# Who issues one block's decay spread, and in which order one DMA queue loads weights and inputs, in a fused Mamba-2 and ELU kernel

## The chip, the cores and the metric

The kernel runs on one core of a Trainium2 chip. The metric is the device time of one execution in microseconds (us), taken over several executions; the median counts. Lower is better.

## The reference, cut to what matters

```python
# attention part: batch 4, 8 heads, 768 tokens, head_dim 32, d_state 16
log_a = np.log(np.clip(a, 1e-06, 1.0))
...
cum = np.cumsum(la, axis=-1)                         # within a chunk
L = np.exp(cum[:, :, :, None] - cum[:, :, None, :]) * causal
CB = np.einsum('bhin,bhjn->bhij', Cc, Bc)
y_intra = np.einsum('bhij,bhjd->bhid', CB * L, xc)
y_inter = np.einsum('bhin,bhnd->bhid', Cc, state) * np.exp(cum)[:, :, :, None]
y[:, :, sl] = y_intra + y_inter
state = decay_full * state + sum over the chunk of B x decay_from_j
...
# feed-forward part: x is y as (3072 tokens, 256), w_in (256, 2048), w_out (2048, 256)
h = x @ w_in
g = np.where(h > 0.0, h, np.exp(np.minimum(h, 0.0)) - 1.0)
return g @ w_out
```

The two weight matrices come in as 64-bit floats and are turned into 32-bit ones on the chip.

## The kernel before, in words

**Tiling.** The 3072 tokens are cut into twelve blocks of 256, counted from 0 in the code (so the code's block 2 is the third). Each block goes through the attention part (decays, scores, states, output `yT`), then through the first product `l1(n, i)` with eight pieces of `w_in`, the ELU, and the second product `l2(n, i)` with eight pieces of `w_out`. From block 4 on, pairs of blocks go through a scheme with fewer products. PSUM has seven rotating buffers (`p_a`, line 76) for scores, transposes and first products, and one more (`p_o`).

**Order.** The schedule is written out by hand (`manual_schedule`, line 82): each engine, and each DMA queue, runs its instructions in the order of the program text. Lines 867 to 1004 are the start of the kernel, where the first three blocks, the conversion of the weight pieces and the loads are interleaved. Nearly all DMAs are issued by SyncE's queue (SP in the profile), so a DMA that waits, or is slow to issue, holds up those after it in the text.

**Weights.** `w_load(i)` (lines 157 to 160) loads piece i, 512 KB, on SP; pieces 0 to 7 are `w_in`, 8 to 15 `w_out`, in eight rotating buffers. `w_take(i, low)` (line 855) reads the raw piece: an Abs on ScalarE (line 175), a scaling (line 182 on ScalarE or 184 on VectorE), a sign mask on VectorE (line 193). `w_give(i)` finishes it with two VectorE steps (lines 201 and 208) and a sum on GpSimd (line 218), after which `l1` or `l2` can use the piece.

**Decays.** Blocks 0 and 1 get their decays from products on TensorE. For the other blocks the running sums of log a, the tile `F`, are stored to DRAM by `write_flat` (lines 325 to 328: two DMAs to `flat`, one to `flat_exp`) and read back. `spread_cum(n)` (lines 348 to 355) broadcasts block n's running sums over the partitions with two DMAs of 256 KB into the tile `L`; it must wait for `flat`. `spread_exp(n)` (lines 357 to 362) does the same with `flat_exp`, one DMA of 128 KB into `ec`. `decay_of(n, h)` (lines 476 to 486) then turns `L` into decays with two exponentials on ScalarE (line 479), and masks them on GpSimd every fourth head (line 484). `load_bc(n)` loads B and C of a block in four DMAs of 64 KB (line 129) and `load_x(n)` its x in two of 128 KB (line 137).

**Around the change.** In the text, piece 4 is loaded at line 872; then lines 921 to 931 issue, on SP: piece 5, the stores of `write_flat`, piece 6, `spread_cum(2)`, piece 7, B and C of block 2, x of block 2, `spread_exp(2)`, pieces 8 and 9. On ScalarE the ELU of line 951 is followed by `w_take(4, nc.scalar)` (line 956), the `yT` copies of block 1 in `inside(across(1), 1)` (line 958; the copies are line 610 on ScalarE and 608 on VectorE), the ELU of line 963 and then the loop of lines 968 to 1004. That loop interleaves, per step s, one first product, `decay_of(2, s)` for s up to 7, the next weight piece (every second step) and one ELU. After step 5 it turns B and C of block 2 (`turn(2)`, `turn_exp(2)`: copies and masks of lines 391, 394 and 402), and at step 7 it computes the scores of block 2 (line 499), whose four PSUM buffers come free when those copies and the ELUs before them are done.

Of the kernel before, what the change touches and what calls it, by code (L numbers as in the profile page):

```python
# [28 lines left out]
def kernel(  # L29
# [27 lines left out]
    nc = tc.nc  # L57
# [21 lines left out]
    def psum(shape, name):  # L79
        return p_a.tile(shape, F32, tag="a", name=name)  # L80
# [21 lines left out]
    def rows_of(n):  # L102
        b, g = place(n)
        return slice(NG * NH * b + g, NG * NH * (b + 1), NG)

    def load_bc(n, c_queue=nc.sync):
        b, g = place(n)
        st.setdefault(n, {})["bc"] = raw.tile([P, 2, 2, NH, N], F32, tag="bc", name="bc", bufs=2)
        if n > 3:
            st[n]["b"] = raw.tile([P, 2, NH, N], F32, tag="b", name="b_tok", bufs=2)  # L110
            for u in range(2):
                sl = slice((2 * g + u) * P, (2 * g + u + 1) * P)
                nc.sync.dma_start(
                    out=st[n]["b"][:, u], in_=B[b, :, sl, :].rearrange("h s n -> s h n"))


            squares = st[n]["bc"].rearrange("p k u h n -> p k (u h n)").rearrange(
                "p k (m r) -> p k m r", m=2)
            for k, src in enumerate((B, C)):
                for m in range(2):  # L120
                    nc.sync.dma_start(
                        out=squares[:, k, m],
                        in_=src[b, m:NH:2, g * BLK:(g + 1) * BLK, :].rearrange(
                            "q (c t) n -> q c (t n)", t=8))
            return
        for u in range(2):
            sl = slice((2 * g + u) * P, (2 * g + u + 1) * P)
            for k, src in enumerate((B, C)):
                (nc.sync, c_queue)[k].dma_start(  # L129
                    out=st[n]["bc"][:, k, u], in_=src[b, :, sl, :].rearrange("h s n -> s h n"))  # L130

    def load_x(n):
        b, g = place(n)
        st[n]["x"] = raw.tile([P, 2, NH * D], F32, tag="xr", name="xr", bufs=4)
        for u in range(2):
            sl = slice((2 * g + u) * P, (2 * g + u + 1) * P)
            nc.sync.dma_start(  # L137
                out=st[n]["x"][:, u].rearrange("p (h d) -> p h d", d=D),
                in_=x[b, :, sl, :].rearrange("h s d -> s h d"))
# [17 lines left out]
    def w_load(i):  # L157
        if i < len(pieces):
            w_raw[i] = conv.tile([P, 2, 2 * CW], U32, tag="w64", name="w64", bufs=W_AHEAD)
            nc.sync.dma_start(out=w_raw[i], in_=pieces[i][1])  # L160
# [11 lines left out]
    def w_abs(i):  # L172
        w_mag[i] = (ffn.tile([P, 2, CW], U32, tag="tmp", name="mag", bufs=1) if i == 2 else
                    conv.tile([P, 2, CW], U32, tag="mag", name="mag"))
        nc.scalar.activation(w_mag[i].bitcast(F32), w_words(i)[1].bitcast(F32), ACT.Abs)
# [4 lines left out]
    def w_low(i, eng):  # L180
        if eng is nc.scalar:
            eng.activation(pieces[i][0], w_words(i)[0], ACT.Identity, scale=2.0 ** -51, bias=two)
        else:
            eng.tensor_scalar(
                out=pieces[i][0], in0=w_words(i)[0], scalar1=2.0 ** -51, scalar2=2.0,
                op0=ALU.mult, op1=ALU.add)
# [3 lines left out]
    def w_sign(i, cols=slice(None)):  # L190
        if i not in w_sgn:
            w_sgn[i] = conv.tile([P, 2, CW], U32, tag="sgn", name="sgn")
        nc.vector.tensor_scalar(  # L193
            out=w_sgn[i][:, :, cols], in0=w_words(i)[1][:, :, cols], scalar1=0x80000000,
            scalar2=None, op0=ALU.bitwise_and)

    def w_high_a(i, cols=slice(None)):
        mag = w_mag[i][:, :, cols]


        nc.vector.tensor_scalar(
            out=mag.bitcast(F32), in0=mag.bitcast(F32),
            scalar1=high_word_as_f32(0x38000000), scalar2=high_word_as_f32(0x47EFFFFF),
            op0=ALU.max, op1=ALU.min)
# [120 lines left out]
    def write_flat():  # L325
        for v in range(2):
            nc.sync.dma_start(out=flat[v], in_=F[:, 0, :, Q * v:Q * v + Q])
        nc.sync.dma_start(out=flat_exp, in_=F[:, 1].rearrange("r u i -> r (u i)"))
# [16 lines left out]
    state = {}  # L345
    starts = {}

    def spread_cum(n):

        st.setdefault(n, {})["L"] = L = att.tile([P, NH, 2, Q], F32, tag="L", name="L", bufs=2)  # L350
        for v in range(2):
            nc.sync.dma_start(
                out=L[Q * v:Q * v + Q].rearrange("p h u i -> p h (u i)"),
                in_=flat[v, rows_of(n)].rearrange("h u i -> h (u i)").unsqueeze(
                    0).to_broadcast([Q, NH, P]))

    def spread_exp(n):

        st.setdefault(n, {})["ec"] = ec = att.tile([P, 2, P], F32, tag="ec", name="ec", bufs=4)
        nc.sync.dma_start(  # L360
            out=ec.rearrange("p u i -> p (u i)"),
            in_=flat_exp[rows_of(n)].unsqueeze(1).to_broadcast([NH, N, BLK]))
# [142 lines left out]
    def weigh(n, q):  # L505
        s = st[n]
        M = att.tile([P, 2, 2, Q], F32, tag="M", name="M", bufs=8)
        nc.vector.tensor_tensor(
            out=M, in0=s["g"][q],
            in1=s["L"][:, 2 * q:2 * q + 2].rearrange("p k u i -> p u k i"), op=ALU.mult)  # L510
        s["M"].append(M)
# [105 lines left out]
    def l1(n, i, parts=1):  # L617

        ps = psum([P, 2, BLK], "ps_h")
        for j in range(2):  # L620
            m = 2 * i + j
            for part in range(parts):
                toks = slice(part * BLK // parts, (part + 1) * BLK // parts)
                for k in range(KC):
                    nc.tensor.matmul(  # L625
                        out=ps[:, j, toks], lhsT=w_in[:, k, m * P:(m + 1) * P],
                        rhs=yT[n // 2][:, k, n % 2].rearrange("p u i -> p (u i)")[:, toks],
                        start=(k == 0), stop=(k == KC - 1))
        lag.append((n, i, ps))
# [10 lines left out]
    def elu():  # L640
        if not begun:
            begin_elu()
        n, i, ps = lag.pop(0)
        e = begun.pop()
        nc.scalar.activation(e, e, ACT.Exp, scale=-1.0)  # L645
        g_of[n, i] = ffn.tile([P, 2, BLK], F32, tag=f"g{n % 2}", name="g", bufs=12)
        nc.vector.scalar_tensor_tensor(  # L647
            out=g_of[n, i], in0=e, scalar=1.0, in1=ps,
            op0=ALU.subtract, op1=ALU.max)
# [205 lines left out]
    def w_take(i, low):  # L855

        w_abs(i)
        w_low(i, low)
        w_sign(i)
# [58 lines left out]
    w_sign(2)  # L918
    w_give(2)
    elu()  # L920
    w_load(5)
    nc.scalar.activation(F[:, 1], F[:, 0], ACT.Exp)
    write_flat()
    w_load(6)
    spread_cum(2)
    w_load(7)
    load_bc(2)
    load_x(2)
    spread_exp(2)
    w_load(8)  # L930
    w_load(9)
    first_low(1, p_o)
# [20 lines left out]
    weigh(1, 2)  # L953
    weigh(1, 3)
    l1(0, 3)
    w_take(4, nc.scalar)
    w_high_a(4)
    inside(across(1), 1)
# [9 lines left out]
    for s, (n, i) in enumerate((  # L968
# [19 lines left out]
        if s == 8:  # L988
            spread_cum(3)
            load_x(3)  # L990
            spread_exp(3)
            weigh(2, 2)
            weigh(2, 3)

            st[0] = kept
            sums(2, 0, pool=p_o, tag="o", parts=(None, last))
            states(0, last)
            st.pop(0)
            states(2)
        if s == 10:  # L1000
            spread_cum(4)
            inside(across(2), 2)
# [197 lines left out]
    n = NP - 2  # L1200
# [41 lines left out]
```

## Time and profile before

| | us |
|---|---|
| median of 3 runs | 357.2 |
| lowest and highest of them | 357.05 and 357.94 |
| the profiled execution, its own time | 359.15 |
| its span on the core | 357.4 |
| PE (TensorE products) busy | 349.0 (98%) |
| DVE (VectorE) busy | 241.3 (67%) |
| POOL (GpSimd) busy | 231.1 (65%) |
| ACT (ScalarE) busy | 200.9 (56%) |

All times in the profile are microseconds from the start of the span. The granted TensorE clock is full throughout. A row of the timeline view has the start, the duration, the engine, the line of the kernel, the operation, the tile written and those read, and how many instructions were merged into the row; brackets give how long the engine sat idle before it, and what ended that. `SPq` and `ACTq` are the two queues that issue DMAs; their rows show the issuing of a DMA, not the flow of its data. A row of the waits view has who waited for whom, the sum, the number of waits and the longest.

### The profile page before, as it was taken

How to read it: one execution, taken by the hardware profiler on the slowest of the kernel's cores; microseconds unless marked ns; L12 is line 12 of the kernel's file. 1: busy time of each engine (PE TensorE's matmuls, PEld its weight loads, DVE VectorE, ACT ScalarE, POOL GpSimd, SP SyncE). 2: the span in 40 equal slices, each digit the busy share in tenths (PEclk: the TensorE clock that was granted, in tenths of full speed). 3: DMA queues.
4: the chain of work that ended last, by engine and by line, in shares of the span. 5: the costliest groups of instructions: out<-in, count | busy, mean ns of one | idle time of the engine just before them, and what ended most of it. 6: DMA issues, size and time to landing. Idle time of an engine off the chain costs nothing.

```text
span 357.4 us, 9940 instructions
## 1 busy us (share of the span) xinstructions
PE 349.0 (98%) x3960; PEld 313.3 (88%) x3960; DVE 241.3 (67%) x500; ACT 200.9 (56%) x491; POOL 231.1 (65%) x365
## 2 busy tenths in 40 slices
PE   8799899999999999999999999999999999999995
PEld 5578688888888999899999999999899999999995
DVE  4996996994799768784577685586685465656212
ACT  4776969867625476635586635486635444434000
POOL 5552553564766998769568769568669545465983
PEclk9999999999999999999999999999999999999999
DMA  8887998380450500046600047500000100000001
GB/s 139 214 249 148 205 327 177 79 141 31 61 147 3 119 0 3 8 89 130 134 0 2 8 72 148 132 5 0 2 2 4 59 3 0 2 0 31 30 2 60
DMA packets 82878, 26.49 MB, mean 74 GB/s; under 512 B 59728, under 2 KB 78736, under 8 KB 82832
## 3 DMA queue, kind: packets, MB, share of 16 engines
q1 hardware_dynamic: 80656, 25.67, 32.0%
q8 instruction: 31, 0.51, 0.6%
q10 hardware_dynamic: 2176, 0.20, 0.5%
q14 instruction: 15, 0.12, 0.1%
HBM read 22.51 MB, written 3.34 MB: 72 GB/s over the span
## 4 chain that ended last, share of the span: by engine, by line
PE 90%; SPq 4%; DVE 2%; DMA 1%; ACT 1%; issue 0%; POOL 0%; DVEq 0%; ACTq 0%
PE ps_o L807 35%; PE ps_h L697 27%; PE ps_h L625 13%; PE ps_o L746 8%; PE ps_y L593 2%; SPq L129 2%; PE ps_g L499 2%; PE ps_y L574 1%; DMA w<-in_moe_w_in_dram 1%; PE ps_st L529 1%; DVE g L647 1%; SPq L160 1%; SPq L137 0%; SPq L88 0%; DVE sgn L193 0%
## 5 line engine op out<-in xcount | busy, mean ns | idle before, releaser
L638 ACT ACTIVATE e<-ps_h 128x512 f32<-128x512 f32 x96 | 57.0, 593 | 91.1 <-DVE ps_h L722 44.1
L807 PEld LDWEIGHTS ps_o<-w_out,g 128*128 128x128 f32 x640 | 79.9, 192 | 3.1 <-issue 0.5
L807 PE MATMUL ps_o<-w_out,g 128*128 128x128 f32 x640 | 80.9, 275 | 0.0
L647 DVE SCALAR_TENSOR_TENSOR g<-e,ps_h 128x512 f32<-128x512 f32 x96 | 65.1, 679 | 11.5 <-ACT e L645 11.5
L625 PE MATMUL ps_h<-yT,w_in 128*128 128x256 f32 (+1 forms) x272 | 60.9, 371 | 2.6 <-POOL w_in L218 2.6
L645 ACT ACTIVATE e<-e 128x512 f32<-128x512 f32 x96 | 61.0, 635 | 2.0
L774 POOL TENSOR_TENSOR g<-g 128x256 f32<-128x256 f32 x33 | 23.9, 726 | 54.5 <-DVE g L647 54.4
L625 PEld LDWEIGHTS ps_h<-yT,w_in 128*128 128x128 f32 x272 | 48.3, 190 | 10.3 <-POOL w_in L218 3.9
L807 PE MATMUL ps_o<-w_sum,g 128*128 128x128 f32 x320 | 42.9, 275 | 0.0
L479 ACT ACTIVATE L<-L,ncum 128x64 f32<-128x64 f32 x160 | 41.0, 337 | 3.0 <-DMA L<-flat 3.0
L807 PEld LDWEIGHTS ps_o<-w_sum,g 128*128 128x128 f32 x320 | 41.1, 192 | 1.2
L697 PE MATMUL ps_h<-yT,w_in 128*128 128x256 f32 x128 | 38.8, 385 | 0.0
L730 DVE TENSOR_TENSOR ps_h<-ps_h,u_sum 128x512 f32<-128x512 f32 x32 | 22.3, 698 | 23.5 <-PE ps_h L697 23.4
L697 PE MATMUL ps_h<-y_sum,w_in 128*128 128x256 f32 x128 | 38.1, 380 | 0.0
L697 PE MATMUL ps_h<-y_sum,w_sum 128*128 128x256 f32 x128 | 38.1, 380 | 0.0
L484 POOL TENSOR_SCALAR_AFFINE_SELECT L<-L 64x512 f32<-64x512 f32 x40 | 28.6, 714 | 10.9 <-ACT L L479 9.6
L714 DVE TENSOR_TENSOR u_sum<-ps_h,u_sum 128x512 f32<-128x512 f32 x32 | 22.1, 690 | 14.5 <-ACT u_sum L707 8.1
L722 DVE TENSOR_TENSOR ps_h<-ps_h,u_sum 128x256 f32<-128x256 f32 x32 | 13.8, 432 | 26.3 <-PE ps_h L697 26.3
L746 PE MATMUL ps_o<-w_out,g 128*128 128x256 f32 x128 | 30.8, 384 | 0.0
L762 POOL TENSOR_TENSOR t<-g 128x256 f32<-128x256 f32 x40 | 28.9, 752 | 0.3
L762 POOL TENSOR_TENSOR g<-g,t 128x256 f32<-128x256 f32 x40 | 28.8, 752 | 0.2
L762 POOL TENSOR_TENSOR g<-t,g 128x256 f32<-128x256 f32 x40 | 27.9, 731 | 1.1 <-PE ps_o L807 1.1
(109 smaller groups left out, 531.9 us busy)
## 6 DMA issues: line engine op xcount, KB each, us to landing
L<-flat SPq DMA_DIRECT2D x20, 256.0 KB
w<-in_moe_w_in_dram SPq DMA_DIRECT2D x8, 512.0 KB
w<-in_moe_w_out_dram SPq DMA_DIRECT2D x8, 512.0 KB
xr<-in_x_dram SPq DMA_DIRECT2D x24, 128.0 KB
out_dram<-c_sum SPq DMA_DIRECT2D x10, 256.0 KB
bc<-in_B_dram SPq DMA_DIRECT2D x24, 64.0 KB
bc<-in_C_dram SPq DMA_DIRECT2D x22, 64.0 KB
ec<-flat_exp SPq DMA_DIRECT2D x10, 128.0 KB
```

Of the source, the lines that this page charges most:

```text
L479: nc.scalar.activation(L[:, h, u], L[:, h, u], ACT.Exp, bias=ncum[:, u, row:row + 1])
L484: nc.gpsimd.affine_select(out=part, in_=part, pattern=[[0, 4], [0, 2], [1, Q]], compare_op=ALU.is_ge, fill=0.0, base=0, channel_multiplier=-1)
L625: nc.tensor.matmul(out=ps[:, j, toks], lhsT=w_in[:, k, m * P:(m + 1) * P], rhs=yT[n // 2][:, k, n % 2].rearrange("p u i -> p (u i)")[:, toks],
L638: nc.scalar.activation(begun[0], lag[0][2], ACT.Relu, scale=-1.0)
L645: nc.scalar.activation(e, e, ACT.Exp, scale=-1.0)
L647: nc.vector.scalar_tensor_tensor(out=g_of[n, i], in0=e, scalar=1.0, in1=ps, op0=ALU.subtract, op1=ALU.max)
L697: nc.tensor.matmul(out=out, lhsT=lhsT, rhs=rhs, start=first, stop=True, skip_group_check=True)
L730: nc.vector.tensor_tensor(out=c2, in0=c2, in1=u[:, 0:2], op=ALU.add)
L746: nc.tensor.matmul(out=o_of[n][:, ts], lhsT=g_of[n, j][:, m % 2, ts * P:(ts + 1) * P], rhs=w_out[:, m], start=(m == 0 and ts == 0), stop=( ...
L762: nc.gpsimd.tensor_tensor(out=out, in0=in0, in1=in1, op=ALU.subtract)
L774: eng.tensor_tensor(out=b12, in0=b12, in1=b11, op=ALU.subtract)
L807: nc.tensor.matmul(out=ps[:, ts], lhsT=b[:, ts * P:(ts + 1) * P], rhs=a[:, i], start=(i == chunk[0] and ts == 0), stop=(i == chunk[-1]), s ...
```

## The change

The spread of block 2's running sums is issued from ScalarE's queue, and stands in the text after `l1(0, 3)` instead of between pieces 6 and 7. `spread_exp(2)` moves to the same place but stays on SP, so that there it comes after piece 9. The stores of `write_flat` come ahead of piece 5; piece 6 still comes ahead of B and C of block 2, and piece 7 now after that block's x. The SP order thus becomes: piece 4, stores, piece 5, piece 6, B and C of block 2, x of block 2, pieces 7, 8 and 9, `spread_exp(2)`, B and C of block 3.

```diff
-    def spread_cum(n):
+    def spread_cum(n, queue=nc.sync):
...
         for v in range(2):
-            nc.sync.dma_start(
+            queue.dma_start(
...
     elu()
-    w_load(5)
     nc.scalar.activation(F[:, 1], F[:, 0], ACT.Exp)
     write_flat()
+    w_load(5)
     w_load(6)
-    spread_cum(2)
-    w_load(7)
     load_bc(2)
     load_x(2)
-    spread_exp(2)
+    w_load(7)
     w_load(8)
     w_load(9)
     first_low(1, p_o)
...
     l1(0, 3)
+    spread_cum(2, nc.scalar)
+    spread_exp(2)
     w_take(4, nc.scalar)
     w_high_a(4)
     inside(across(1), 1)
```

## The prediction

> **What bounds the kernel now.** I read the page first: PE is busy for 98% of the span, so only the few places where TensorE waits can give anything. The waits view of PE over the whole run ends with three rows, and from 55 us on it has none: what TensorE gains or loses before 55 us reaches the end one for one. So I read the waits between 18 and 56 us:
>
> ```profile
> ACT L L479 <- DMA L<-flat: 3.0, 1, 3.0
> ...
> PEld ps_g L499 <- ACT e L638: 1.5, 2, 1.2
> ...
> PE ps_g L499 <- DVE ctm L394: 0.8, 1, 0.8
> ...
> PE ps_h L625 <- POOL w_in L218: 0.6, 2, 0.4
> ```
>
> ScalarE waits 3.0 us for block 2's running sums to land. TensorE waits at that block's scores (line 499), and a little for a weight piece. The timeline of PE shows where and how long:
>
> ```profile
> 38.69 1.89 PE L625 MATMUL ps_h<-yT,w_in 128*128 128x256 f32 x8
> 40.97 1.99 PE L625 MATMUL ps_h<-yT,w_in 128*128 128x256 f32 x8 [0.39 <-POOL w_in L218]
> 43.79 1.51 PE L499 MATMUL ps_g<-ctm,bct 32*64 32x128 f32 x32 [0.82 <-DVE ctm L394]
> 45.23 1.99 PE L625 MATMUL ps_h<-yT,w_in 128*128 128x256 f32 x8
> ```
>
> Undisturbed, a first product takes 1.73 us from start to start (56.28 to 58.01) and 32 score products 0.62 (block 3's: 65.45 to 66.07). So the last row could start at 38.69 + 2 x 1.73 + 0.62 = 42.77. It starts at 45.23: **2.46 us** can be won, no more. Why are the scores late? The timeline of ACT:
>
> ```profile
> 22.88 0.63 ACT L645 ACTIVATE e<-e 128x512 f32<-128x512 f32 x1
> 23.41 0.66 ACT L175 ACTIVATE mag<-w 128x512 f32<-128x512 f32 x1
> 23.97 0.75 ACT L182 ACTIVATE w_in<-w,two 128x512 f32<-128x512 uint32 x1
> 26.62 0.81 ACT L610 COPY yT<-ps_y 128x128 f32<-128x128 f32 x3 [1.90 <-PE ps_y L593]
> 27.45 0.60 ACT L638 ACTIVATE e<-ps_h 128x512 f32<-128x512 f32 x1
> 28.08 0.63 ACT L645 ACTIVATE e<-e 128x512 f32<-128x512 f32 x1
> 31.72 1.06 ACT L479 ACTIVATE L<-L,ncum 128x64 f32<-128x64 f32 x4 [3.01 <-DMA L<-flat]
> ```
>
> From 31.72 to 47.9 ScalarE has no gap in its timeline: it carries the 3 us as a backlog. VectorE takes its work from it (g and the weight masks), and the scores' four PSUM buffers and `ctm` come from VectorE, g of (1, 3) last, at 44.58. Why does the spread land at 31.72? The issues on SP:
>
> ```profile
> 16.31 3.79 SPq L160 DMA_DIRECT2D w<-in_moe_w_in_dram  x2
> 20.21 1.33 SPq L327 DMA_DIRECT2D flat<-F  x2
> 21.64 0.54 SPq L328 DMA_DIRECT2D flat_exp<-F  x1
> 22.24 0.46 SPq L160 DMA_DIRECT2D w<-in_moe_w_in_dram  x1
> 24.32 2.41 SPq L352 DMA_DIRECT2D L<-flat  x2
> 26.78 0.97 SPq L160 DMA_DIRECT2D w<-in_moe_w_in_dram  x1
> ```
>
> The stores are queued behind pieces 4 and 5 (the first issue is held until 19.59), SP then waits until 24.32 for them to land, and issues the two spreads in 2.41. From the last issue's end (26.73) to ScalarE's start is 5.0 us.
>
> **What the Trainium skill says.** "Perfetto Trace Analysis", section on the HWDGE DMA instruction: its semaphore wait is on the sequencer, and the descriptor generator is then locked while it is used. So ScalarE's stream stops at the spread until `flat` has landed and both are issued. The same page, section on DVE and Act instructions: the sequencer pushes an ACTIVATE into a wait queue and goes on. The trace agrees: a DMA was issued on ACT's queue at 1.74 while its table load ran from 1.71 to 2.99. "DMA: Bandwidth & Descriptors", section "Issuing engines are not separate DMA queues": another issuer saves only its sequencer's issue time, the data share the same 16 engines. No row of before tests this beyond the start. The same page, "Queues, rings and completion order": an engine takes turns between the queues that have work. So the spread would no longer stand behind piece 6 but share with pieces 5 and 6.
>
> **The change part by part.**
>
> *Stores ahead of piece 5.* Their source is ready (the sums precede the exponential, which ends at 17.3), so SP issues them at 19.7 to 21.0, then `flat_exp` to 21.6. Before, the landing came 2.8 us after their issue ended (21.54 to 24.32), with 512 KB of piece 5 ahead; at the 315 to 389 KB per us that the DMA engines moved from 21 to 24 us this is some 1.5 us, if all of it was still to flow. So `flat` is there between 21.0 + 1.3 = 22.3 and 21.0 + 2.8 = 23.8; I take 23.2.
>
> *Spread on ScalarE's queue.* Two issues of the spread row's median 0.63 us each: 23.2 to 24.5. Line 175 starts at 24.5 instead of 23.41, 1.1 us later, and ends at 25.2, line 182 at 25.8. Behind them stand the `yT` copies at 26.62, ahead of which ScalarE sat idle for 1.90: the 1.1 is hidden. VectorE's step on piece 4 starts at 26.42 and needs line 175 at 25.2: hidden too. **Cost 0**, as long as the issues end by about 25.3. If they take as long as the slow spread before (0.73 and 1.68), they end at 25.6, and cost 0.3. If SP's stall on the third B/C DMA of block 2 (3.05 us in before) holds the generator for both queues, ACT comes free near 27.5 and the cost is 27.5 - 25.3 = 2.2. Below nothing it can't be: nothing in this stretch of TensorE waits on the queue. I take 0 and keep 2.2.
>
> *When L lands.* 24.5 + 5.0 (before's delay) = 29.5. The bounds: 2.8 (the stores' delay) gives 27.3; if pieces 5 and 6, 1 MB, all flow ahead of it, 1.5 us more gives 31.0. I take 29.5: ScalarE's wait shrinks from 3.0 to 0.8, so its work starts 2.2 us earlier.
>
> *What is late next.* ScalarE copies the transposed B of block 2 at 40.87; TensorE writes it from 38.25 for 0.38, ending at 38.63. So ScalarE can be early by no more than 40.87 - 38.63 = 2.2 there, even if L came sooner. Shifting g of (1, 3) from 44.58 by 2.2 gives 42.4 (TensorE gets there at 42.15), and g of (0, 5), which frees the buffer for the next first product, from 45.16 to 43.0. The product at 45.23 thus starts at 43.0: **gain 2.2 us**. The wait for a weight sum (0.39) goes with it.
>
> *Piece 5 later.* Issued at 21.7 to 22.2 instead of 19.6 to 20.1, landing near 25 to 26; VectorE reads it at 29.60. 0. If it were 4 us later than that, VectorE would start on it late, but its next step waits for ScalarE at 30.4 anyway.
>
> *B, C and x of block 2 earlier, piece 7 later.* SP no longer spends 1.6 us waiting and 2.41 issuing. B, C and x took 6.8 us of issue before (27.85 to 34.65), so now some 22.7 to 29.7. Piece 7 is issued near 30 instead of 26.8 and lands by 35; its first reader on VectorE moves from 40.59 to about 38.4. 0, with 3 us to spare. Uncovered, each us beyond would delay the `w_in` sum of piece 7, used at TensorE's 45.5.
>
> *`spread_exp(2)` behind pieces 7, 8 and 9.* Issued at some 31 to 36 (34.70 before); with 1.5 MB ahead, at most 4.5 us to flow, it lands by 36 to 41. Its reader, VectorE's line 402, moves from 43.56 to 41.4. 0. At the late end this takes up all the slack.
>
> The sum is 0 - 2.2 = **-2.2 us**. The profiled execution took 359.15 (span 357.4 and 1.75 around it), so it would be 356.95; it stands 1.95 above the median 357.2. The same 2.2 off the median gives **355.0**.
>
> **The rivals.**
>
> *A, as worked out, 0.60.* 355.0, from 354.7 (all 2.46) to 355.6 (0.3 of cost and L 0.3 late).
>
> *B, the wait only shrinks, 0.14.* L shares the DMA engines with pieces 5 and 6 and lands at 30.7: ScalarE gains 1.0, the scores come 1.0 earlier, 356.2. For it: the data rate is 348 to 377 KB per us at 23 to 25 us, so the engines are nearly full then. Against it: at 25 to 26 it falls to 160.
>
> *C, slower, 0.15.* ScalarE's queue is held by SP's: the lock stays with SP through B and C of block 2, which need about 5 us from 22.7, until 27.9. The spreads are then issued until 29.2, so line 175 starts at 29.2 instead of 25.3 at the latest, and TensorE's first product of block 1 (27.48) slips by 3.9. Of that, 2.46 is absorbed by the waits that go: +1.4, 358.6. It decides for slower once the issues end later than 25.3 + 2.46 = 27.8, and then L, at 29.2 + 5.0 = 34.2, is later than before as well. For it: SP's issues stall in just this stretch. Against it: at the start, between 1.70 and 3.0 us, SP and ACT issued two DMAs each at 0.39 to 0.58, with no stall.
>
> *D, no difference, 0.11.* The same hold, but for SP's one stall (27.5): 2.2 lost ahead of block 1, 2.2 won at the scores, 357.2.
>
> **How the numbers follow.** A measurement tells 0.3% (1.07 us) from no change, so faster means below 356.13. A gives 0.60; half of B, which lies on the border, 0.07: 0.67. Slower (above 358.27) is C: 0.15. The rest, D and half of B and what lies between, 0.18. Range: A's low end less 0.4 for the spread between runs, 354.3, to 357.5, which takes in B and D and leaves out C and a few more.
>
> **What would show it.** A issue row of L352 on ACTq near 23 to 24.5; ScalarE's wait before line 479 below 1 us; the score products in about 0.7 us from start to start, starting near 42.2; and the product after them near 43.0. TensorE's first product of block 1 should still start at 27.5. If that slips, C or D is at work; if it holds and ScalarE still waits over 1.5 us for L, it is B. The prediction would also be wrong if TensorE waited anew for a piece or for `ec` between 40 and 55 us.

## The result, and the profile after

The changed kernel takes **362.88 us** (median of 6 runs, 360.82 to 364.18) against 357.45 for the kernel before in the same comparison: a ratio of **1.0139**, 95% interval 1.0105 to 1.0173. It is slower by some 5 us, where a gain of 2.2 was forecast. A later comparison on another chip gave 361.91 and 1.0121 (1.0098 to 1.0145). The profiled execution took 362.95 (span 361.2).

The waits of the changed kernel between 10 and 60 us, longest of those that matter:

```profile
ACT mag L175 <- DMA bc<-in_B_dram: 5.2, 1, 5.2
...
PE ps_h L625 <- ACT yT L610: 4.3, 2, 3.3
...
ACT L L479 <- DMA L<-flat: 1.4, 1, 1.4
```

The wait for L did shrink. In its place ScalarE stands still for 5.2 us ahead of line 175, and TensorE then waits 3.3 us for `yT`. The view names a B DMA as what ended ScalarE's wait, although line 175 reads weight piece 4: what stands ahead of line 175 in ScalarE's stream is the spread. Its timeline:

```profile
22.97 0.63 ACT L645 ACTIVATE e<-e 128x512 f32<-128x512 f32 x1
26.65 2.11 ACTq L352 DMA_DIRECT2D L<-flat  x2
28.81 0.66 ACT L175 ACTIVATE mag<-w 128x512 f32<-128x512 f32 x1 [5.21 <-DMA bc<-in_B_dram]
29.37 0.75 ACT L182 ACTIVATE w_in<-w,two 128x512 f32<-128x512 uint32 x1
30.02 0.79 ACT L610 COPY yT<-ps_y 128x128 f32<-128x128 f32 x3
30.83 0.60 ACT L638 ACTIVATE e<-ps_h 128x512 f32<-128x512 f32 x1
```

The spread was to be issued from 23.2 to 24.5; it is issued from 26.65 to 28.76. Line 175 starts at 28.81 and the `yT` copies at 30.02, with no gap between them: they come late because of the queue alone. SyncE's issues in the same stretch:

```profile
18.83 1.33 SPq L327 DMA_DIRECT2D flat<-F  x2
...
20.85 0.93 SPq L160 DMA_DIRECT2D w<-in_moe_w_in_dram  x2
21.89 0.40 SPq L129 DMA_DIRECT2D bc<-in_B_dram  x1
22.34 0.58 SPq L129 DMA_DIRECT2D bc<-in_C_dram  x1
22.97 3.39 SPq L129 DMA_DIRECT2D bc<-in_B_dram  x1
```

The stores go out at 18.83 to 20.16, as early as forecast. The third B/C DMA is held for 3.39 us until 26.36, which is suspiciously near 26.65. TensorE:

```profile
30.86 13.22 PE L625 MATMUL ps_h<-yT,w_in 128*128 128x128 f32 x64 [3.30 <-ACT yT L610]
43.92 0.38 PE L387 MATMUL ps_tb<-ident,bc 128*128 128x128 f32 x2
...
47.91 0.69 PE L499 MATMUL ps_g<-ctm,bct 32*64 32x128 f32 x32
48.53 1.99 PE L625 MATMUL ps_h<-yT,w_in 128*128 128x256 f32 x8
```

The 64 products, 10.93 us before, take 13.22. Two rows of the view by stretches, whose columns after the busy times end in the granted clock, the DMA share and GB/s, say why:

```profile
29.00:30.00 1.00, 0.00 (x0) 0.00 (x0) 0.43 (x2) 1.00 (x2) 0.00 (x0) 0.63 1.25 201
31.00:32.00 1.00, 1.00 (x5) 1.00 (x6) 1.00 (x3) 0.97 (x2) 0.33 (x1) 0.50 1.13 193
```

While TensorE stands idle its granted clock falls to one half. It is back at full only after 36 us (0.96 from 36 to 37, 1.00 from 37).

**What the spread waited for.** The trace also records every increment of the DMA completion semaphores, and the program as built says which one each DMA uses. There are eight of them, given to the DMAs of both queues in turn, and each DMA waits until the DMA eight before it in that round has landed:

```
the spread's   round in the    DMA eight before            its last    spread's
DMA            changed kernel  in the round                increment   issue
first          34              26, weight piece 6          26.63       26.65
second         36              28, first C of block 2      28.16       28.18
                               (the two stores of flat:    22.28 and 22.46)
```

The stores had landed when ScalarE got there, at 22.98. Nothing else was missing but the landing of piece 6, and then of a C, neither of which the spread reads.

### The profile page after: what moved, and what is told of

The parts are those of the page before. It is cut to its first block, busy times and chain, and to the rows that moved or that the text cites. A ratio compares the mean times of both kernels' runs of the same rounds, so it can differ in the third digit from the quotient of the medians.

```text
span 361.2 us, 9938 instructions
## 1 busy us (share of the span) xinstructions
PE 350.3 (97%) x3960; PEld 315.4 (87%) x3960; DVE 241.8 (67%) x500; ACT 201.2 (56%) x491; POOL 231.6 (64%) x365
## 4 chain that ended last, share of the span: by engine, by line
PE 92%; DMA 3%; SPq 1%; ACT 1%; DVE 1%; POOL 0%; issue 0%; ACTq 0%
PE ps_o L807 35%; PE ps_h L697 27%; PE ps_h L625 15%; PE ps_o L746 8%; PE ps_y L593 2%; DMA bc<-in_C_dram 2%; PE ps_g L499 2%; DMA w<-in_moe_w_in_dram 2%; PE ps_y L574 1%; PE ps_st L529 1%; SPq L129 0%; POOL w_in L218 0%; ACT mag L175 0%; SPq L137 0%; DVE mag L208 0%
## 5 line engine op out<-in xcount | busy, mean ns | idle before, releaser
L625 PE MATMUL ps_h<-yT,w_in 128*128 128x256 f32 (+1 forms) x272 | 63.0, 383 | 5.7 <-ACT yT L610 4.3
L625 PEld LDWEIGHTS ps_h<-yT,w_in 128*128 128x128 f32 x272 | 50.8, 203 | 12.9 <-ACT yT L610 3.5
```

Source lines behind the costliest of these rows:

```text
L625: nc.tensor.matmul(out=ps[:, j, toks], lhsT=w_in[:, k, m * P:(m + 1) * P], rhs=yT[n // 2][:, k, n % 2].rearrange("p u i -> p (u i)")[:, toks],
```

## The experiments

Theory 1: ScalarE's stream stands still until the previous user of the spread's completion semaphore has landed. Theory 2, rival C of the prediction: SyncE's held B/C DMA keeps the descriptor generator from ScalarE. Both fit the first issue in this one trace, since 26.36 and 26.63 are so near.

**Other turns in the round.** The order on both queues stays that of the change; only the turns move:

```diff
     states(1)
+    st[2]["x"] = raw.tile([P, 2, NH * D], F32, tag="xr", name="xr", bufs=4)
+    for u in range(2):
+        nc.gpsimd.memset(st[2]["x"][0:32, u, 0:8], 0.0)
...
     spread_cum(2, nc.scalar)
+    load_x(2)
+    w_load(7)
+    w_load(8)
+    w_load(9)
     spread_exp(2)
```

(the four loads are taken out of their place ahead of `first_low(1, p_o)`; `load_x` uses the tile made here)

> The changed kernel, with both queues in the same order, but x of block 2 and what follows it held back by two tiny GpSimd writes, so that in the round of the eight DMA completion semaphores the two spread DMAs follow the stores of the running sums and not piece 6 and block 2's C. Theory 1 (ScalarE's DMA waits until the previous user of its completion semaphore has landed): the spreads are issued near 23.0 to 24.4 although SyncE's third B/C DMA is stalled from 23 to 26.4; yT is in time, TensorE's first product of block 1 starts at 27.5 at full clock, and the time is near 355.2, about 0.6% below the kernel before. Theory 2 (SyncE's stalled DMA holds the descriptor generator for both queues): the spreads still wait until about 26.4, and the time stays near 362.

It took 358.23, a ratio of 1.0025 (1.0014 to 1.0036). The spread's predecessors in the round are now the second store of `flat` and the store of `flat_exp` (last increments at 22.83 and 23.08). ACT's and SP's timelines of this kernel:

```profile
24.08 1.35 ACTq L353 DMA_DIRECT2D L<-flat  x2
25.47 0.67 ACT L176 ACTIVATE mag<-w 128x512 f32<-128x512 f32 x1 [0.83 <-issue]
...
31.82 1.06 ACT L480 ACTIVATE L<-L,ncum 128x64 f32<-128x64 f32 x4 [1.97 <-DMA L<-flat]
```

```profile
23.35 3.45 SPq L129 DMA_DIRECT2D bc<-in_B_dram  x1
```

ScalarE issues both spreads between 24.08 and 25.43, in the middle of the 3.45 us in which SyncE's B DMA is held. Theory 2 falls; theory 1 stands. By the ratios, 1.0139 and 1.0025, it has some four fifths of the loss; the rest is still clear of no change, and this experiment doesn't say what it is. (In this execution everything is about 1.1 us late from 20 us on: TensorE's clock stood at one half from 15 to 17 us, long before the spread, as it does in the profile of the order with the spread on SP, below, where that product starts at 28.51. So the first product of block 1 at 28.61 is no loss of the change.) The hoped-for gain isn't there either: L is usable 6.4 us after the last issue, where 5.0 had been assumed.

**The stores alone.** The kernel before with `w_load(5)` moved behind `write_flat()`:

> The kernel before with one part of the change alone: the stores of the running sums ahead of piece 5; the spread stays on SyncE's queue. Both theories put the loss on ScalarE's queue, so none is expected here: flat lands near 22.5, the spread is issued at 22.5 to 24.5, ScalarE's wait for L shrinks from 3.0 to about 1, and the time is near 355.5. A third theory, that the new order of the loads costs the time (piece 5 late), says about 360 or more.

358.08, ratio 1.0013 (1.0001 to 1.0025): next to no loss, but no gain, where 355.5 was expected. Its trace does what was forecast: spread issued from 21.21 to 22.53 on SP, ScalarE's wait for L 0.34, scores without a stall.

```profile
29.60 1.06 ACT L479 ACTIVATE L<-L,ncum 128x64 f32<-128x64 f32 x4 [0.34 <-DMA L<-flat]
```

So this part of the change does what it should and the time doesn't move. That puts the 2.46 us that were to be won in doubt; the kernel before is profiled twice more below.

**The queue alone.**

```diff
     w_load(6)
-    spread_cum(2)
     w_load(7)
...
     l1(0, 3)
+    spread_cum(2, nc.scalar)
     w_take(4, nc.scalar)
```

> The kernel before with the other part alone: the spread on ScalarE's queue at the place of the change, all loads in the order of before. In the round of the semaphores the two spreads now follow C of block 2 and its x, which land at about 29 and 32. Theory 1: ScalarE issues the second spread only near 32, block 1's first product starts near 34 to 35 and the time is 365 to 368, worse than with the whole change. Theory 2: the issue waits for SyncE's stalled third B/C DMA, which ends near 29 to 31 here, so a time near 363 to 365.

368.09 (4 runs), ratio 1.0297 (1.026 to 1.0334), at the upper end of theory 1.

```profile
28.29 2.77 ACTq L352 DMA_DIRECT2D L<-flat  x2
31.11 0.66 ACT L175 ACTIVATE mag<-w 128x512 f32<-128x512 f32 x1 [7.45 <-DMA xr<-in_x_dram]
```

The spread's DMAs are issued at 28.29 and 30.45; C of block 2 had its last increment at 28.27, the first half of x at 30.43. SyncE's held B/C DMA had ended at 26.58, 1.7 us before the first of them, so here too theory 2 doesn't fit. TensorE's first product of block 1 starts at 33.16. The other parts of the change had put DMAs that land earlier (26.63 and 28.16) eight places before the spread, and so lessened what the queue costs.

**TensorE kept busy in the gap.**

```diff
     eb = turned(E, "eb", 1.0, nc.vector)
+    ps_warm = p_o.tile([P, 4, P], F32, tag="o", name="ps_warm")
+    for _ in range(3):
+        nc.tensor.matmul(
+            out=ps_warm, lhsT=ident, rhs=ident.unsqueeze(1).to_broadcast([P, 4, P]),
+            start=True, stop=True)
     elu()
```

> The changed kernel with three products of 512 columns on the identity, whose result nobody reads, on TensorE ahead of block 1's first product, while it waits for yT. They add work, and take none of the wait away. If TensorE's halved clock after the gap is a part of the loss, the clock stays at full, the 64 products take 10.9 instead of 13.2, ScalarE's backlog then sets the scores, and the time falls by about 1.5, to 361.4. If the clock is no part of it, the time stays or rises by up to 0.5.

361.77 (359.49 to 364.23, 6 runs). The clock stayed at full and the 64 products took 10.64. Because six runs don't tell 1 us here, it was repeated beside the changed kernel, with six runs of each:

> The changed kernel once more, in more runs and on the same chip as the next one: 362 to 363. In its profile ScalarE's first spread is again issued just when piece 6 has landed, the second when block 2's first C has, and TensorE's 64 products of block 1 take over 12 us at a halved clock.

> The changed kernel with the three unread products in TensorE's gap once more, in more runs: if the halved clock is a part of the loss, the time lies 0.7 to 1.5 below the changed kernel's, with the 64 products in 10.6 to 11; if not, the two agree within 0.3.

361.91 (ratio 1.0121, 1.0098 to 1.0145) and 361.08 (1.0126, 1.0093 to 1.0159): the medians lie 0.8 apart, but the ratios and their intervals are nearly the same. The clock's part is plain in the traces (12.08 against 10.64 for the 64 products) and **not settled in the time**. In the two profiles with the unread products a part of what the full clock wins is lost again later. In the second, the 32 score products take 1.45 in place of 0.69. In the first, TensorE stands still inside block 2's products of line 593, for a reason that the view doesn't show ("issue"):

```profile
54.15 0.35 PE L593 MATMUL ps_y<-M,xr 64*32 64x64 f32 x17 [1.50 <-issue]
```

The semaphore again tells the issue to 0.02 us: last increments at 25.36 and 27.00, issues at 25.38 and 27.02 in the one; 25.48 and 27.96, issues at 25.50 and 27.98 in the other.

**The kernel before, twice more.**

> The kernel before, profiled once more. The first profile's execution (359.15) lay above all 43 runs of before on the other chip (356.62 to 358.74). Theory A (the 3.0 us wait for L and the 2.46 us at the scores are there in every execution): again about 3 us before line 479, the product after the scores again some 2.4 later than TensorE alone would allow. Theory B (they belong to that execution): the wait for L is 1.5 us or less, and less than 1 us is lost at the scores.

> The kernel before, profiled a third time, for the spread between executions; as for the second: theory A about 3 us of wait for L and 2.4 lost at the scores, theory B well below that.

Theory B holds in both. The second profile (358.06) and the third (357.43, closest to the median) have these ACT rows, one from each:

```profile
30.27 0.82 ACT L479 ACTIVATE L<-L,ncum 128x64 f32<-128x64 f32 x3 [1.01 <-DVE g L647]
```

```profile
30.06 1.06 ACT L479 ACTIVATE L<-L,ncum 128x64 f32<-128x64 f32 x4 [1.26 <-DMA L<-flat]
```

(In the second, too, it was L that came last: the last increment of its spread is at 30.17.) The third's TensorE:

```profile
27.57 10.93 PE L625 MATMUL ps_h<-yT,w_in 128*128 128x128 f32 x64
...
38.77 3.62 PE L625 MATMUL ps_h<-yT,w_in 128*128 128x256 f32 x16
42.32 1.31 PE L499 MATMUL ps_g<-ctm,bct 32*64 32x128 f32 x32
43.56 1.99 PE L625 MATMUL ps_h<-yT,w_in 128*128 128x256 f32 x8
```

From the first product of block 1 to the one after the scores it takes 15.99 here, 15.74 in the second profile and 17.75 in the first; with no stall (the stores alone) it takes 15.37. So these two executions lose **0.4 to 0.6 us** there, and the first lost 2.4. It is a rare one: its 359.15 lies above all 43 runs of one comparison (356.62 to 358.74), and 2 of the 35 of another come up to it (359.14 and 359.20). The kernel with other turns takes 16.69, with L late again.

**The order of the change, with the spread on SP.** `spread_cum(2)` behind `w_load(6)`, all else as changed:

> The changed kernel with the queue alone undone: the spread of block 2 on SyncE's queue right behind piece 6, the stores ahead of piece 5, piece 7 behind x, the spread of the exponentials behind piece 9. With ScalarE's queue free of DMAs the whole loss should be gone: between 357.0 and 358.2, as with the stores moved alone (358.08). A theory in which the late piece 7 or the late ec costs time says 359 or more.

357.39, ratio 0.9998 (0.9983 to 1.0013). The late piece 7 and the late `ec` cost nothing that shows; the whole loss comes with the spread on ScalarE's queue, in these turns of the round. L is in time here, without a gain: the 15.37 of the stores alone come back, and the time is that of the kernel before.

**No spread at all**, meant as the bound of the gain:

```diff
-    spread_cum(2)
...
     states(1)
+    st[2]["L"] = att.tile([P, NH, 2, Q], F32, tag="L", name="L", bufs=2)
+    nc.gpsimd.memset(st[2]["L"], 0.0)
```

> The kernel before without the spread of block 2: its L is filled with zeros on GpSimd (so block 2's decays are left out, and its output is another one) and nothing waits for a DMA there. It is the bound of what an earlier landing of L can give. Theory A (2.46 us lost at the scores in every execution): about 355.0 to 355.3. Theory B (a typical execution loses little there): 356.5 to 357.3.

358.99, ratio 1.0035 (1.002 to 1.0051): a miss of both theories. The fill, put on GpSimd, is no free stand-in. While it runs (26.89 to 27.84), VectorE's sign mask of line 193 takes 0.96 (0.42 in the kernel with the order on SP); the `yT` copies behind it are late, block 1's products stop after two of the 64, and the transposes of block 2 start 0.40 later than in that kernel (39.67 against 39.27). The larger part of this profile's delay is another: TensorE stands still for 0.95 us inside the products of line 593, for a reason that the view doesn't show. So the run bounds nothing. What does are the three profiles of before, and the two kernels in which L came early (the stores alone, and the order with the spread on SP): neither is faster.

## Why the prediction was wrong, point by point

*"ScalarE's stream stops at the spread until `flat` has landed and both are issued"* is the step that failed, and the sum of "Spread on ScalarE's queue" with it. `flat` landed at 22.46, earlier than the 23.2 taken, and the two issues took 0.66 and 0.58, as taken. But the DMAs had a third thing to wait for, the previous user of their completion semaphore: the sum put that wait at nothing, and it took from 22.98 to 26.65 for the first DMA and from 27.37 to 28.18 for the second. The ends that this part reckoned with (24.5, 25.6 and 27.5) left out the one that came, 28.76. Rival C's 29.2 was near it by luck, through a mechanism that the runs refute. That the kernel before had no such trouble proves nothing: on SP this wait stands in a queue that only issues DMAs, on ScalarE it stands in front of compute.

*Cost 0, hidden in the 1.90 us of idle time.* The reasoning on cover was right, and named the point: from 25.3 on each us of delay is one of TensorE's. 28.76 - 25.3 = 3.5; TensorE's start slipped from 27.57 (third profile of before) to 30.86, 3.29.

*"Of that, 2.46 is absorbed"* (rival C) failed twice. Only about 0.6 could be absorbed, and the gap brought a cost that no rival had: the halved clock, 13.22 - 10.93 = 2.29. The Trainium skill says it, in "TensorE: Matmul & The Clock Gate", section "What's actually happening": the array's clock is gated to one half after an idle window of about 3.4 us, a window that runs free of the kernel. This trace agrees on the half, but shorter gaps were enough: with TensorE idle from 27.56 on, the clock fell some 1.7 us later (0.63 in the stretch from 29 to 30) and stayed low for about 6.8 us, and in the repeat, whose whole gap was 2.37 us, it stayed low for about 3.4.

The sum from the two profiles nearest their medians, 357.43 and 362.95: first product +3.29, its 64 products +2.29, and from the turns of block 2 to the product after the scores 4.61 in place of 5.23, -0.62. Together **+4.96** at 48.5 us, and 5.17 at TensorE's end: it is carried to the end about one for one, as forecast. This is the account of these two traces; what the clock's 2.29 is worth in the medians is what the runs with the unread products left open. The remaining 0.3 of the 5.5 between the spans and times lies behind TensorE's last products.

*"2.46 us can be won"* failed as a size, so that the gain would not have come even with no cost of the queue. It was read from one execution which, as the prediction noted, stood 1.95 above the median; the same 2.2 was then taken off the median. An execution that is 2 us above the others may be so because of just the wait that one reads. Two more profiles put the prize at 0.4 to 0.6, below the 1.07 us that the prediction says a measurement tells.

*When L lands.* The 5.0 us of delay was no constant: from the last issue's end to line 479 it was 4.7 in the changed kernel, 6.4 with the other turns and 7.1 with the stores alone, against 4.5 from the issue's end at 25.55 in the third profile of before. Sharing the DMA engines with other loads fits this; that it is the cause is argued, not shown, and whether the two queues took turns, as the prediction has it, no run here isolates.

*Piece 5, piece 7, B and C, `spread_exp` late or early: 0 each.* Right: none shows as a wait of TensorE, and that order with the spread on SP costs nothing (0.9998).

*What would show it.* The prediction said that a slip of the first product would mean rival C or D. The place was right, C's mechanism (a held generator) was not: the kernel with other turns issues on ScalarE's queue while SyncE's issue is held, so the lock that the prediction cites did not act from one queue on the other here.

## What to carry to other kernels

A DMA moved to a queue that also computes brings all its waits along, and one of them may not be in the kernel's text: the DMA a fixed number of places before it in a round of completion semaphores. List what the built program makes each DMA wait for before putting it ahead of compute, and ask when that lands. And read the wait that a change is to remove in more than one profile, above all when the profiled execution is slower than the usual run.

## What the runs showed of the hardware that was not expected

A DMA issue that waits for a completion semaphore starts 0.02 us after its last increment (nine of the twelve spread issues on ScalarE in the six profiles that have them; the tenth, the second of the kernel with TensorE kept busy, followed 0.06 after its increment, as the first issue ended only at 26.61, and the two of the kernel with other turns were not waiting). The sixteen increments of one DMA don't come together: those of block 2's first C came between 26.46 and 27.39, but for the last, at 28.16, and the second spread waited for that one.

The clock also goes with the spread between executions. Of the 43 runs of the kernel before in one comparison, the 12 with a mean granted clock of 0.994 or 0.995 have a median of 357.9, the other 31 (0.998 to 1.0) one of 357.4. One stretch of 3.4 us at half clock would give about 0.995 (an estimate: half of 3.4 over the span of 356), and four of the profiles, that with the order on SP among them, have such a stretch at about 14 to 18 us.
